# Softmax rows divided on GpSimd before the transposes, in a fused attention and two-layer MLP kernel with a planned instruction order

## The chip, the cores and the metric

The kernel runs on one core of a Trainium2 chip. A core has five engines with an instruction queue each: PE (TensorE: matmuls and transposes), DVE (VectorE), ACT (ScalarE), POOL (GpSimd) and SP (here it only issues DMAs). Each queue runs in order and the queues wait for each other by semaphores. The metric is device time in microseconds (us), lower is better.

## The reference, cut to what matters

```python
def _attn_ref(q, k, v):                        # batch 2, 12 heads, 448 tokens, head size 64
    scores = scale * np.matmul(q, k.transpose(0, 1, 3, 2))
    scores = np.where(mask, -1000000000.0, scores)          # causal
    scores = scores - np.max(scores, axis=-1, keepdims=True)
    attn = np.exp(scores)
    attn = attn / (np.sum(attn, axis=-1, keepdims=True) + 1e-09)
    return np.matmul(attn, v).astype(np.float32)

def reference(**kwargs):
    attn_out = _attn_ref(**attn_kwargs)
    x = attn_out.transpose(0, 2, 1, 3).reshape(B * S, H * D)          # 896 x 768
    x = _moe_ref(x=x, **moe_kwargs)      # (rational function of x @ w_in) @ w_out, 2048 wide
    return _moe2_ref(x=x, **moe2_kwargs) # (sigmoid(x @ w_gate) * (x @ w_val)) @ w_out, 1536 wide
```

All of it is float32, apart from weights that the kernel reads as double words and rounds itself.

## The kernel before, in words

**Attention.** Heads are taken two at a time: 12 pairs n = 0 to 11, six of each batch. The 448 query rows of a head are four tiles t of 112 rows, and a pair is worked off in three groups k: tiles 0 and 1, tile 2, tile 3. For each group PE multiplies queries by keys (`scores`, tile `s`, in PSUM), DVE takes the masked, negated row maximum and writes the scaled scores to SBUF (`maximum`, tile `e`, one instruction for each head of the pair), ACT makes the exponentials in place with the row sums beside them (`exponentials`, tile `sum`), PE transposes the 112 x 112 blocks (`turn`, tile `p`), DVE or ACT copies them from PSUM to SBUF (`copied`, tile `pt`), and PE multiplies them by the values (`values`, tile `x`). The tiles `s` and `p` share one ring of two PSUM buffers (`ps_s`), so each waits for the readers of the one before the last. A tile `e` has two buffers, one for each head, so `maximum` of pair n + 1 waits for the transposes of pair n.

**The softmax division before.** The exponentials are transposed and multiplied undivided. `inverses` turns the eight columns of `sum` of a pair into reciprocals on DVE, `factors` spreads them over PSUM with eight matmuls on PE (tile `r`, line 501), `factors_out` copies that tile to SBUF on ACT (line 511), and `result` multiplies `x` by it on DVE (line 528). Then ACT rounds the product to `xh` and the rest goes to `xl`: on POOL for ten pairs, on DVE for the last pair of each batch (line 540). `xh` and `xl` are what the MLP reads.

**The MLP.** Each product is made of three matmuls (high by high, low by high, high by low). Of the first layer the tiles `h` (x by w_in) and `o` (by w_out) of batch 0 stand between the attention's instructions on PE as filler: a tile `h` needs `xh` and `xl` of pair u for its u-th part. A weight portion of 128 x 768 comes by DMA (`raw`), passes two ACT steps, one of DVE (`val`, line 164) and two of POOL (`wh` or `oh`, line 172; `wl` or `ol`, line 176). From 130 us on, only MLP matmuls run on PE.

**What sets the order.** Every piece of work is a `Job` with an engine, a cost, what it depends on and a rank. `in_turn` plays the jobs through with these costs (an engine that comes free takes the ready job of lowest rank), and the kernel's instructions are put on each engine in that order, which is then fixed:

```python
        now, e = min((max(free[e], min(j.ready for j in w)), e) for e, w in waiting.items() if w)
        job = min((j for j in waiting[e] if j.ready <= now), key=lambda j: j.rank)
        waiting[e].remove(job)
        free[e] = now + job.cost
```

Of the kernel before, what the change touches and what calls it, by code (L numbers as in the profile page):

```python
# [8 lines left out]
F32 = mybir.dt.float32  # L9
# [16 lines left out]
class Job:  # L26


    def __init__(self, engine, cost, deps, rank, emit):
        self.engine, self.cost, self.rank, self.emit = engine, cost, rank, emit  # L30
        self.deps = deps
        self.ready = 0.0
        self.then = []


def in_turn(named, handoff):

    free = {}
    waiting = {}
# [30 lines left out]
def tile_causal_attention__moe_rational__moe_glu(  # L70
# [13 lines left out]
    nc = tc.nc  # L84
# [408 lines left out]

    def factors(n):

        d = T[n]
        d["r"] = ps_r.tile([P, 512], F32, tag="r", name=f"r_{n}")[:, :S]

        for i in range(NQ):
            for j in range(2):  # L500
                nc.tensor.matmul(
                    d["r"][j * D : (j + 1) * D, i * CP : (i + 1) * CP],
                    d["sum"][:, i, j : j + 1].to_broadcast([CP, D]),
                    ident[:CP, :CP],
                    start=True,
                    stop=True,
                )
# [49 lines left out]
    LA = 2  # L557
    R_TURN, R_R, R_X, R_W = -11.0, -16.0, 34.0, -3.5
    R_MAX, R_COPY, R_INV, R_XN = -14.5, -9.5, 7.0, 12.5
    R_EXP, R_ROUT = 6.25, -42.5  # L560
    W_AT, W_STEP = 9, 5
    R_SUM = 9.5
    EXP = (0.39, 0.48, 0.57, 0.67)
    MAX = (0.28, 0.39, 0.51, 0.62)
    COPY = (0.39, 0.62, 0.70, 1.09)
    both = range(2)
    for it in range(len(pairs) * NG + LA):
        n, k = divmod(it, NG)
        rank = it * NQ / NG
        if n < len(pairs):  # L570
            if k == 0:
                job(("load", n), "SP", 3.0, [("x", n - 3, NQ - 1)], (n - 2) * NQ, load, n)
            job(
                ("s", n, k),
                "PE",
                sum(0.187 * (t + 1) + 0.05 for t in GROUPS[k]) + 0.25,
                [("load", n), *freed_by("s")],
                rank - 37.5,
                scores,
                n,  # L580
                k,
            )
            for t in GROUPS[k]:
                for j in both:
                    job(("max", n, t, j), "DVE", MAX[t] + 0.08, [("s", n, k), ("p", n - 1, k)], rank + R_MAX, maximum, n, k, t, j)
                    job(("exp", n, t, j), "ACT", EXP[t] + 0.19, [("max", n, t, j), ("r", n - 3)], rank + R_EXP, exponentials, n, t, j)
# [15 lines left out]
        for t in GROUPS[k]:  # L602
            job(("copy", n, t), "ACT" if t == 2 else "DVE", COPY[t], [("p", n, k), ("x", n - 2, NQ - 1)], rank + R_COPY, copied, n, k, t)
        freed["s"].append([("copy", n, t) for t in GROUPS[k]])
        if k < NG - 1:
            continue
        job(("inv", n), "DVE", 0.4, [("exp", n, t, j) for t in range(NQ) for j in both], rank + R_INV, inverses, n)
        job(("r", n), "PE", 0.9, [("inv", n), ("r out", n - 1)], rank + R_R, factors, n)
        job(("r out", n), "ACT", 0.52, [("r", n), ("hi", n - 1), ("lo", n - 1)], rank + R_ROUT, factors_out, n)
        for kt in range(NQ):  # L610
            deps = [("copy", n, t) for t in range(kt, NQ)] + [("x", n, kt - 1) if kt else ("xn", n - 1)]
            job(("x", n, kt), "PE", 0.187 * (NQ - kt) + 0.15, deps, rank + R_X + kt / 2, values, n, kt)
        job(("xn", n), "DVE", 0.62, [("x", n, NQ - 1), ("r out", n)], rank + R_XN, result, n)
        job(("hi", n), "ACT", 0.57, [("xn", n)], rank + 1, result_hi, n)
        final = pairs[n][1] == NP - 1
        job(("lo", n), "DVE" if final else "POOL", 0.62 if final else 1.14, [("hi", n)], rank + 1, result_lo, n)


# [24 lines left out]

    STAGES = [("SP", 4.0), ("ACT", 0.92), ("ACT", 0.9), ("DVE", 1.3), ("ACT", 0.84), ("POOL", 2.0)]
    portions = []

    def portion(key, w, free, rank):
        p = len(portions)
        portions.append(key)
        for m, (engine, cost) in enumerate(STAGES):  # L650
# [9 lines left out]
            if not isinstance(rank, tuple):  # L660
                r = rank - 4 if m == 0 else rank + R_W
# [94 lines left out]
    def stage_out(c, b):  # L756
# [23 lines left out]
    def stage_out2(c, b):  # L780
# [113 lines left out]
```

## Time and profile before

| what | value |
|---|---|
| median of 3 runs | 603.45 us (603.12 to 603.87) |
| span of the profiled execution, first to last instruction | 601.4 us |
| PE busy | 593.5 us, 99% |
| DVE, ACT, POOL busy | 358.0 (60%), 357.2 (59%), 254.4 us (42%) |
| PE busy from 0 to 120 us | 115.63 us |
| DVE busy from 60 to 120 us | 54.21 us of 60 |

The profile shows one execution; its page gives the span and no total of its own, so its time is taken as the span and the 2.05 us by which the median exceeds it. The shares of the whole mix two stages: up to about 126 us attention, where four engines are loaded, and after it the MLP, where PE alone is full.

### The profile page before, as it was taken

Reading aid. Unit: us, or ns where it says so; the run is one execution under the profiler, and the core shown is the slowest. Engines: PE = TensorE matmul, PEld = TensorE weight load, DVE = VectorE, ACT = ScalarE, POOL = GpSimd, SP = SyncE. Lnnn points to the kernel's source line nnn. Section 1 sums busy time; section 2 is a strip of 40 time slices with the busy share of each in tenths; the row PEclk is TensorE's granted clock in tenths of the full one; section 3 lists DMA queues with packets and bytes.
Section 4 is the critical chain, followed back from the end, with each engine's and each line's share of the span. In section 5 each row is a group of like instructions: output and inputs, shape, how many; then the busy total and the mean of one; then the engine's idle time right before and its main releaser. Section 6 shows DMA issues by size and latency. Waiting matters only on the chain.

```text
span 601.4 us, 8821 instructions
## 1 busy us (share of the span) xinstructions
PE 593.5 (99%) x3352; PEld 511.6 (85%) x3352; DVE 358.0 (60%) x677; ACT 357.2 (59%) x686; POOL 254.4 (42%) x193
## 2 busy tenths in 40 slices
PE   7999999999999999999999999999999999999997
PEld 5566666689988998898898989989989989989987
DVE  5877899938968986789685243246336335312314
ACT  6888888858897793859396448766344444111010
POOL 0634321357529656534746465545145144211010
PEclk9999999999999999999999999999999999999999
DMA  7645340045413351323421054645324123000004
GB/s 242 207 173 158 118 166 16 6 157 166 146 53 110 108 195 53 113 88 123 152 59 51 2 158 158 210 157 161 102 105 159 54 105 106 0 1 1 0 14 170
DMA packets 25641, 65.05 MB, mean 108 GB/s; under 512 B 1984, under 2 KB 3776, under 8 KB 25600
## 3 DMA queue, kind: packets, MB, share of 16 engines
q1 hardware_dynamic: 25600, 64.50, 32.7%
q8 instruction: 26, 0.43, 0.3%
q14 instruction: 15, 0.12, 0.1%
HBM read 61.74 MB, written 2.75 MB: 107 GB/s over the span
## 4 chain that ended last, share of the span: by engine, by line
PE 97%; DVE 2%; issue 0%; ACT 0%; DVEq 0%
PE h L256 7%; PE o L314 6%; PE h L258 6%; PE h L257 6%; PE o L315 6%; PE o L316 6%; PE z L381 5%; PE z L379 5%; PE z L380 5%; PE gu L257 5%; PE gu L258 5%; PE gu L256 5%; PE vu L257 5%; PE vu L256 5%; PE vu L258 5%; PE s L442 4%
## 5 line engine op out<-in xcount | busy, mean ns | idle before, releaser
L361 POOL TENSOR_TENSOR gl<-pr_u,gh 128x384 fp32r<-128x384 f32 (+1 forms) x24 | 27.7, 1153 | 111.5 <-ACT gh L359 111.5
L289 POOL TENSOR_TENSOR gl_h<-t_h,gh_h 128x384 fp32r<-128x384 f32 (+2 forms) x32 | 39.2, 1226 | 84.0 <-ACT gh_h L287 83.9
L256 PE MATMUL h<-xh,wh_in 128*128 128x384 f32 (+2 forms) x192 | 71.3, 371 | 0.0
L314 PE MATMUL o<-gh_h,oh_out 128*128 128x384 f32 (+2 forms) x192 | 70.3, 366 | 0.0
L315 PE MATMUL o<-gl_h,oh_out 128*128 128x384 f32 (+2 forms) x192 | 69.9, 364 | 0.0
L316 PE MATMUL o<-gh_h,ol_out 128*128 128x384 f32 (+2 forms) x192 | 69.9, 364 | 0.0
L258 PE MATMUL h<-xh,wl_in 128*128 128x384 f32 (+2 forms) x192 | 69.7, 363 | 0.0
L257 PE MATMUL h<-xl,wh_in 128*128 128x384 f32 (+2 forms) x192 | 69.7, 363 | 0.0
L176 POOL TENSOR_TENSOR ol_out<-val_out,oh_out 128x768 fp32r<-128x768 f32 x28 | 55.1, 1971 | 26.7 <-ACT oh_out L174 25.4
L389 DVE TENSOR_TENSOR y<-y,z 128x384 f32<-128x384 f32 x70 | 38.3, 552 | 32.2 <-PE z L381 32.1
L357 DVE TENSOR_TENSOR pr_u<-sg_u,vu 128x384 f32<-128x384 f32 (+1 forms) x24 | 14.8, 617 | 70.8 <-PE vu L258 68.4
L381 PE MATMUL z<-oh_out,gl 128*128 128x384 f32 x168 | 56.2, 335 | 0.0
L379 PE MATMUL z<-oh_out,gh 128*128 128x384 f32 x168 | 56.2, 335 | 0.0
L380 PE MATMUL z<-ol_out,gh 128*128 128x384 f32 x168 | 56.2, 334 | 0.0
L164 DVE SCALAR_TENSOR_TENSOR val_out<-raw_out 128x768 uint32<-128x768 uint32 x28 | 35.7, 1277 | 31.3 <-ACT raw_out L161 23.4
L464 ACT ACTIVATE e<-e,sc 112x112 f32<-112x112 f32 (+3 forms) x96 | 49.7, 522 | 6.5 <-DVE sc L450 6.3
L258 PE MATMUL gu<-xh,wl_gate 128*128 128x384 f32 (+1 forms) x144 | 52.2, 363 | 0.0
L257 PE MATMUL gu<-xl,wh_gate 128*128 128x384 f32 (+1 forms) x144 | 52.2, 363 | 0.0
L257 PE MATMUL vu<-xl,wh_val 128*128 128x384 f32 (+1 forms) x144 | 52.1, 362 | 0.0
L256 PE MATMUL gu<-xh,wh_gate 128*128 128x384 f32 (+1 forms) x144 | 52.1, 362 | 0.0
L256 PE MATMUL vu<-xh,wh_val 128*128 128x384 f32 (+1 forms) x144 | 52.1, 362 | 0.0
L258 PE MATMUL vu<-xh,wl_val 128*128 128x384 f32 (+1 forms) x144 | 52.1, 362 | 0.0
(89 smaller groups left out, 1425.5 us busy)
## 6 DMA issues: line engine op xcount, KB each, us to landing
raw_out<-in_moe_w_out_dram SPq DMA_DIRECT2D x28, 768.0 KB, 4.3
raw_in<-in_moe_w_in_dram SPq DMA_DIRECT2D x16, 768.0 KB, 4.5
raw_gate<-in_moe_w_gate_dram SPq DMA_DIRECT2D x12, 768.0 KB, 4.3
raw_val<-in_moe_w_val_dram SPq DMA_DIRECT2D x12, 768.0 KB, 4.3
qk<-in_qk_dram SPq DMA_DIRECT2D x12, 448.0 KB, 5.7
v<-in_v_dram SPq DMA_DIRECT2D x12, 224.0 KB, 3.8
out_dram<-y SPq DMA_DIRECT2D x14, 192.0 KB, 1.8
a_sb<-in_moe_a_dram SPq DMA_DIRECT2D x1, 2.0 KB, 7.1
```

Source lines behind the costliest of these rows:

```text
L176: nc.gpsimd.tensor_tensor(lo, vf, hi, op=ALU.subtract)
L256: nc.tensor.matmul(ps, hi[:, c, fs], xh[:, c, bs], start=(c == 0), stop=False)
L257: nc.tensor.matmul(ps, hi[:, c, fs], xl[:, c, bs], start=False, stop=False)
L258: nc.tensor.matmul(ps, lo[:, c, fs], xh[:, c, bs], start=False, stop=(c == KC - 1))
L289: nc.gpsimd.tensor_tensor(gl, t, gh, op=ALU.subtract)
L314: nc.tensor.matmul(ps, hi[:, es], gh, start=(i == 0), stop=False)
L315: nc.tensor.matmul(ps, hi[:, es], gl, start=False, stop=False)
L316: nc.tensor.matmul(ps, lo[:, es], gh, start=False, stop=(i == NF - 1))
L379: nc.tensor.matmul(ps, gh[:, ms], hi[:, ns], start=(i == 0), stop=False)
L380: nc.tensor.matmul(ps, gh[:, ms], lo[:, ns], start=False, stop=False)
L381: nc.tensor.matmul(ps, gl[:, ms], hi[:, ns], start=False, stop=(i == NF2 - 1))
L464: nc.scalar.activation(e, e, AF.Exp, bias=d["sc"][:, t, j : j + 1], scale=-1.0, accum_out=d["sum"][:, t, j : j + 1])
```

## The change

The row sums are inverted group by group (`inverses(n, k)`: an addition and a reciprocal for 4, 2 and 2 columns), and a new function `normalised` multiplies each tile `e` in place by its rows' reciprocals on POOL, eight instructions for a pair, before PE transposes it. `factors`, `factors_out` and `result` are gone, `xh` and `xl` are made from the tile `x` in PSUM, `xl` always on DVE. The PSUM that `r` took gives `x` a second buffer. The planner adds a cost (`switch`) where PE goes over between instructions that use half the array's rows (`s`), half its columns (`x`) or all of it, and a rank penalty (`stay`) for doing so; all ranks, costs and handoff times are new.

```diff
-        job = min((j for j in waiting[e] if j.ready <= now), key=lambda j: j.rank)
+        job = min((j for j in waiting[e] if j.ready <= now), key=lambda j: j.rank + stay * (j.mode != mode.get(e)))
         waiting[e].remove(job)
-        free[e] = now + job.cost
+        free[e] = now + job.cost + switch * (job.mode != mode.get(e))
+        mode[e] = job.mode
...
-    ps_x = att.enter_context(tc.tile_pool(name="ps_x", bufs=1, space=PSUM))
-    ps_r = att.enter_context(tc.tile_pool(name="ps_r", bufs=1, space=PSUM))
+    ps_x = att.enter_context(tc.tile_pool(name="ps_x", bufs=2, space=PSUM))
...
-    def inverses(n):
-        rs = T[n]["sum"]
+    def inverses(n, k):
+        rs = T[n]["sum"][:, GROUPS[k][0] : GROUPS[k][-1] + 1]
         nc.vector.tensor_scalar_add(rs, rs, 1e-9)
         nc.vector.reciprocal(rs, rs)
+
+    def normalised(n, t, j):
+        e = T[n]["e", t, j]
+        nc.gpsimd.tensor_scalar(e, e, T[n]["sum"][:, t, j : j + 1], 1.0, op0=ALU.mult, op1=ALU.mult)
...
-    def factors_out(n):
-        T[n]["xn"] = xn_p.tile([P, S], F32, tag="xn", name=f"xn_{n}")
-        nc.scalar.copy(T[n]["xn"], T[n]["r"])
...
-    def result(n):
-        nc.vector.tensor_tensor(T[n]["xn"], T[n]["xn"], T[n]["x"], op=ALU.mult)
...
     def result_hi(n):
-        nc.scalar.copy(xh[x_part(n)], T[n]["xn"])
+        nc.scalar.copy(xh[x_part(n)], T[n]["x"])
 
     def result_lo(n):
-
-        eng = nc.vector if pairs[n][1] == NP - 1 else nc.gpsimd
-        eng.tensor_tensor(xl[x_part(n)], T[n]["xn"], xh[x_part(n)], op=ALU.subtract)
+        nc.vector.tensor_tensor(xl[x_part(n)], T[n]["x"], xh[x_part(n)], op=ALU.subtract)
...
+        job(("inv", n, k), "DVE", 0.31, [("exp", n, t, j) for t in GROUPS[k] for j in both], rank + R["inv"], inverses, n, k)
+        for t in GROUPS[k]:
+            for j in both:
+                job(("norm", n, t, j), "POOL", NORM[t] + C["norm"], [("inv", n, k)], rank + R["norm"], normalised, n, t, j)
         job(
             ("p", n, k),
             "PE",
-            sum(0.2 * (t + 1) for t in GROUPS[k]) + 0.1,
-            [("exp", n, t, j) for t in GROUPS[k] for j in both] + freed_by("s"),
-            rank + R_TURN,
+            sum(0.191 * (t + 1) for t in GROUPS[k]) + C["p"],
+            [("norm", n, t, j) for t in GROUPS[k] for j in both] + freed_by("s"),
+            rank + R["turn"],
```

PE, the start of the attention. In the rows `s_n_k` and `p_n_k` are scores and transposes of pair n, group k (a running number behind), and `e_n_t_j` the exponentials of tile t and head j. Before:

```order
L442 MATMUL s_0_2_178<-qk_0_0_143 112x448 x2
L482 MATMUL p_0_0_194<-ident_102,e_0_0_0_165 112x112
L482 MATMUL p_0_0_194<-ident_102,e_0_0_1_167 112x112
L482 MATMUL p_0_0_194<-ident_102,e_0_1_0_170 112x112 x2
L482 MATMUL p_0_0_194<-ident_102,e_0_1_1_173 112x112 x2
L442 MATMUL s_1_0_206<-qk_0_1_150 112x112 x2
L442 MATMUL s_1_0_206<-qk_0_1_150 112x224 x2
L482 MATMUL p_0_1_215<-ident_102,e_0_2_0_176 112x112 x3
L482 MATMUL p_0_1_215<-ident_102,e_0_2_1_188 112x112 x3
L442 MATMUL s_1_1_236<-qk_0_1_150 112x336 x2
L501 MATMUL r_0_243<-ident_102,sum_0_0_147 64x112 x8
```

The same place on PE in the changed kernel:

```order
L443 MATMUL s_0_2_175<-qk_0_0_140 112x448 x2
L443 MATMUL s_1_0_202<-qk_0_1_147 112x112 x2
L443 MATMUL s_1_0_202<-qk_0_1_147 112x224 x2
L487 MATMUL p_0_0_210<-ident_102,e_0_0_0_162 112x112
L487 MATMUL p_0_0_210<-ident_102,e_0_0_1_164 112x112
L487 MATMUL p_0_0_210<-ident_102,e_0_1_0_167 112x112 x2
L487 MATMUL p_0_0_210<-ident_102,e_0_1_1_170 112x112 x2
L487 MATMUL p_0_1_228<-ident_102,e_0_2_0_172 112x112 x3
L487 MATMUL p_0_1_228<-ident_102,e_0_2_1_178 112x112 x3
L443 MATMUL s_1_1_247<-qk_0_1_147 112x336 x2
```

The scores of pair 1 have moved ahead of the first transposes, and the tile `r` behind `s_1_1` is gone.

DVE, the same stretch. `ISA` rows are row maxima (the ones on `sc` read their result out), `COPY` takes the transposes out of PSUM. Before:

```order
L450 ISA e_0_3_0_192,sc_0_0_148<-s_0_2_178,mask_107 112x448
L450 ISA sc_0_0_148 112x1
L450 ISA e_0_3_1_201,sc_0_0_148<-s_0_2_178,mask_107 112x448
L450 ISA sc_0_0_148 112x1
L492 COPY pt_0_0_149<-p_0_0_194 112x2x112
L492 COPY pt_0_0_149<-p_0_0_194 112x2x2x112
L450 ISA e_1_0_0_222,sc_0_1_155<-s_1_0_206,mask_107 112x112
```

DVE there in the changed kernel:

```order
L471 TENSOR_SCALAR sum_0_0_144<-sum_0_0_144 112x4
L472 RECIPROCAL sum_0_0_144<-sum_0_0_144 112x4
L451 ISA e_0_3_1_194,sc_0_0_145<-s_0_2_175,mask_107 112x448
L451 ISA sc_0_0_145 112x1
L471 TENSOR_SCALAR sum_0_0_144<-sum_0_0_144 112x2
L472 RECIPROCAL sum_0_0_144<-sum_0_0_144 112x2
L471 TENSOR_SCALAR sum_0_0_144<-sum_0_0_144 112x2
L472 RECIPROCAL sum_0_0_144<-sum_0_0_144 112x2
L497 COPY pt_0_0_146<-p_0_0_210 112x2x112
L497 COPY pt_0_0_146<-p_0_0_210 112x2x2x112
L451 ISA e_1_0_0_226,sc_0_1_152<-s_1_0_202,mask_107 112x112
```

The three inversions of pair 0 stand between its last maxima and the copies, and the maxima of pair 1 still stand behind the copies of `p_0_0`.

POOL, where the first weight portions pass, in the changed kernel (before, the rows of `wh` and `wl` followed each other there, with one `xl` behind the second portion):

```order
L476 TENSOR_SCALAR e_1_2_1_264<-e_1_2_1_264,sum_0_1_151 112x336
L174 TENSOR_SCALAR wh_in0_0_312<-val_in0_0_0_301 128x768
L178 TENSOR_TENSOR wl_in0_0_313<-val_in0_0_0_301,wh_in0_0_312 128x768
L476 TENSOR_SCALAR e_1_3_0_286<-e_1_3_0_286,sum_0_1_151 112x448
L476 TENSOR_SCALAR e_1_3_1_291<-e_1_3_1_291,sum_0_1_151 112x448
L174 TENSOR_SCALAR wh_in0_0_312<-val_in0_0_3_349 128x768
L178 TENSOR_TENSOR wl_in0_0_313<-val_in0_0_3_349,wh_in0_0_312 128x768
L476 TENSOR_SCALAR e_2_0_0_326<-e_2_0_0_326,sum_0_2_185 112x112
```

The divisions of the exponentials now share POOL's queue with the weights, in turn. Over the attention as a whole, PE goes over between its three ways of using the array 111 times before and 94 times after; with the `r` tiles struck out of the order before, it is 96.

## Rows read from the trace of the kernel before

**Rows 1.** The page: busy time and share of each engine; the chain that ended last.

```profile
span 601.4 us, 8821 instructions
...
PE 593.5 (99%) x3352; PEld 511.6 (85%) x3352; DVE 358.0 (60%) x677; ACT 357.2 (59%) x686; POOL 254.4 (42%) x193
...
PE 97%; DVE 2%; issue 0%; ACT 0%; DVEq 0%
```

**Rows 2.** Busy time in three stretches: PE, PEld, DVE, ACT, POOL; clock, DMA share, GB/s.

```profile
0.00:20.00 20.00, 16.69 (x124) 11.13 (x124) 11.93 (x53) 14.24 (x40) 3.46 (x11) 1.00 0.60 192
20.00:60.00 40.00, 40.00 (x327) 24.15 (x324) 30.98 (x99) 34.17 (x99) 19.48 (x16) 1.00 0.58 196
60.00:120.00 60.00, 58.94 (x460) 38.13 (x456) 54.21 (x149) 50.49 (x134) 17.03 (x14) 1.00 0.23 77
```

**Rows 3.** Timeline of PE: start, duration, instructions; one `r` tile, and `x` split or whole.

```profile
67.03 0.99 PE L501 MATMUL r<-ident,sum 112*64 112x112 f32 x16
67.95 0.98 PE L482 MATMUL p<-ident,e 112*112 112x112 f32 x8
...
71.18 0.97 PE L519 MATMUL x<-pt,v 112*64 112x448 f32 x4
...
73.57 1.36 PE L519 MATMUL x<-pt,v 112*64 112x336 f32 x12
...
81.13 2.11 PE L519 MATMUL x<-pt,v 112*64 112x448 f32 x16
```

**Rows 4.** Groups by line, 0 to 130 us: count, busy us, mean ns, idle before.

```profile
L501 PE MATMUL r<-ident,sum 112*64 112x112 f32 x192 | 11.8, 266 | 0.1
L528 DVE TENSOR_TENSOR xn<-xn,x 128x448 f32<-128x448 f32 x12 | 7.4, 614 | 2.2 <-PE x L519 1.9 <-ACT xn L511 0.3
L540 POOL TENSOR_TENSOR xl<-xn,xh 128x448 fp32r<-128x448 f32 x10 | 12.9, 1290 | 19.5 <-ACT xh L535 19.5
L176 POOL TENSOR_TENSOR wl_in<-val_in,wh_in 128x768 fp32r<-128x768 f32 x6 | 11.6, 1932 | 0.5
L172 POOL TENSOR_SCALAR wh_in<-val_in 128x768 fp32r<-128x768 f32 x6 | 5.0, 835 | 31.4 <-DVE val_in L164 24.9 <-DMA raw_in<-in_moe_w_in_dram 6.5
```

**Rows 5.** Timeline of PE at the start of the attention, idle time before in brackets.

```profile
7.70 0.78 PE L482 MATMUL p<-ident,e 112*112 112x112 f32 x6
9.04 0.83 PE L442 MATMUL s<-qk 64*112 64x112 f32 x8 [0.56 <-DVE sc L450]
9.97 0.76 PE L482 MATMUL p<-ident,e 112*112 112x112 f32 x6
```

**Rows 6.** Timeline of DVE in the same stretch.

```profile
8.36 0.62 DVE L450 CUSTOM_DVE_ANT_0 e<-s,mask 112x448 f32<-112x448 f32 x1
...
8.91 0.92 DVE L492 COPY pt<-p 112x224 f32<-112x224 f32 x2
10.04 0.28 DVE L450 CUSTOM_DVE_ANT_0 e<-s,mask 112x112 f32<-112x112 f32 x1 [0.21 <-PE s L442]
...
11.05 0.17 DVE L470 TENSOR_SCALAR sum<-sum 112x8 f32<-112x8 f32 x1
...
11.37 0.12 DVE L624 TENSOR_SCALAR nb<-b_sb 128x2 f32<-128x2 f32 x1
```

**Rows 7.** Timelines of POOL and DVE at 64 us, the same moment.

```profile
64.45 1.83 POOL L176 TENSOR_TENSOR ol_out<-val_out,oh_out 128x768 fp32r<-128x768 f32 x1
...
64.54 1.77 DVE L470 TENSOR_SCALAR sum<-sum 112x8 f32<-112x8 f32 x1
```

**Rows 8.** Timelines of DVE, PE and POOL behind the attention, 125 to 149 us.

```profile
125.37 0.63 DVE L540 TENSOR_TENSOR xl<-xn,xh 128x448 fp32r<-128x448 f32 x1 [1.14 <-ACT xh L535]
...
134.06 0.37 PE L256 MATMUL h<-xh,wh_in 128*128 128x448 f32 x1
...
136.52 1.85 POOL L176 TENSOR_TENSOR wl_in<-val_in,wh_in 128x768 fp32r<-128x768 f32 x1
...
148.94 0.34 PE L256 MATMUL h<-xh,wh_in 128*128 128x384 f32 x1
```

More of the change, by code (lines that the diff above doesn't have):

```diff
@@ L26, with __init__ @@
 class Job:
-    def __init__(self, engine, cost, deps, rank, emit):
-        self.engine, self.cost, self.rank, self.emit = engine, cost, rank, emit
+    def __init__(self, engine, cost, deps, rank, emit, mode=None):
+        self.engine, self.cost, self.rank, self.emit, self.mode = engine, cost, rank, emit, mode
         self.deps = deps
@@ L33, in __init__, with in_turn @@
         self.then = []
-def in_turn(named, handoff):
+def in_turn(named, handoff, switch, stay):
     free = {}
+    mode = {}
     waiting = {}
@@ L492, in copied @@
             nc.vector.tensor_copy(dst, src)
[L494 to L507, printed above, removed]
-    def factors_out(n):
-        T[n]["xn"] = xn_p.tile([P, S], F32, tag="xn", name=f"xn_{n}")
-        nc.scalar.copy(T[n]["xn"], T[n]["r"])
     def values(n, kt):
@@ L557, in tile_causal_attention__moe_rational__moe_glu @@
     LA = 2
[L558 to L565, printed above, removed]
+    R = dict(s=-36.0, turn=-8.0, x=31.0, w=-5.0, max=-13.0, copy=-9.0, inv=-12.5, lo=20.0, norm=-4.0, hi=2.5, exp=8.25, sum=7.5)
+    C = dict(w_at=14.0, w_step=6.0, s=0.05, p=-0.08, x=-0.03, max=0.05, exp=0.07, switch=0.19, stay=1.0, norm=0.0, copy=0.12, wa=-0.02)
+    H = dict(PE=0.19, DVE=0.13, ACT=0.14, POOL=0.15, SP=0.15)
+    MODES = {"s": "rows", "x": "columns"}
+    EXP = (0.37, 0.465, 0.56, 0.65)
+    MAX = (0.195, 0.31, 0.425, 0.54)
+    NORM = (0.2, 0.32, 0.45, 0.57)
+    COPY = (0.30, 0.53, 0.60, 1.0)
     both = range(2)
@@ L575, in tile_causal_attention__moe_rational__moe_glu @@
                 "PE",
-                sum(0.187 * (t + 1) + 0.05 for t in GROUPS[k]) + 0.25,
+                sum(0.187 * (t + 1) + 0.0 for t in GROUPS[k]) + C["s"],
                 [("load", n), *freed_by("s")],
-                rank - 37.5,
+                rank + R["s"],
                 scores,
@@ L584, in tile_causal_attention__moe_rational__moe_glu @@
                 for j in both:
-                    job(("max", n, t, j), "DVE", MAX[t] + 0.08, [("s", n, k), ("p", n - 1, k)], rank + R_MAX, maximum, n, k, t, j)
-                    job(("exp", n, t, j), "ACT", EXP[t] + 0.19, [("max", n, t, j), ("r", n - 3)], rank + R_EXP, exponentials, n, t, j)
+                    job(("max", n, t, j), "DVE", MAX[t] + C["max"], [("s", n, k), ("p", n - 1, k)], rank + R["max"], maximum, n, k, t, j)
+                    job(("exp", n, t, j), "ACT", EXP[t] + C["exp"], [("max", n, t, j), *[("norm", n - 3, t, i) for i in both]], rank + R["exp"], exponentials, n, t, j)
             freed["s"].append([("max", n, t, j) for t in GROUPS[k] for j in both])
@@ L602, in tile_causal_attention__moe_rational__moe_glu @@
         for t in GROUPS[k]:
-            job(("copy", n, t), "ACT" if t == 2 else "DVE", COPY[t], [("p", n, k), ("x", n - 2, NQ - 1)], rank + R_COPY, copied, n, k, t)
+            job(("copy", n, t), "ACT" if t == 2 else "DVE", COPY[t] + C["copy"], [("p", n, k), ("x", n - 2, NQ - 1)], rank + R["copy"], copied, n, k, t)
         freed["s"].append([("copy", n, t) for t in GROUPS[k]])
@@ L606, in tile_causal_attention__moe_rational__moe_glu @@
             continue
-        job(("inv", n), "DVE", 0.4, [("exp", n, t, j) for t in range(NQ) for j in both], rank + R_INV, inverses, n)
-        job(("r", n), "PE", 0.9, [("inv", n), ("r out", n - 1)], rank + R_R, factors, n)
-        job(("r out", n), "ACT", 0.52, [("r", n), ("hi", n - 1), ("lo", n - 1)], rank + R_ROUT, factors_out, n)
         for kt in range(NQ):
[L611 to L616, printed above, removed]
+            deps = [("copy", n, t) for t in range(kt, NQ)] + [("x", n, kt - 1) if kt else ("lo", n - 2)]
+            job(("x", n, kt), "PE", 0.187 * (NQ - kt) + C["x"], deps, rank + R["x"] + kt / 2, values, n, kt)
+        job(("hi", n), "ACT", 0.42, [("x", n, NQ - 1)], rank + R["hi"], result_hi, n)
+        job(("lo", n), "DVE", 0.53, [("hi", n)], rank + R["lo"], result_lo, n)
     def coefficients():
@@ L642, in tile_causal_attention__moe_rational__moe_glu @@
     UNIT = {S: 0.615, CUT: 0.525, NT - CUT: 0.69}
-    STAGES = [("SP", 4.0), ("ACT", 0.92), ("ACT", 0.9), ("DVE", 1.3), ("ACT", 0.84), ("POOL", 2.0)]
+    STAGES = [("SP", 4.0), ("ACT", 0.79 + C["wa"]), ("ACT", 0.79 + C["wa"]), ("DVE", 1.1), ("ACT", 0.73 + C["wa"]), ("POOL", 1.9)]
     portions = []
@@ L660, in portion @@
             if not isinstance(rank, tuple):
[L661 removed]
+                r = rank - 4 if m == 0 else rank + R["w"]
             job((*key, m), engine, cost, deps, r, _spent, w)
@@ L733, in followed @@
         n_tmp.append((key, len(stages) - 1))
-    RATIONAL = [("ACT", 1.9), ("DVE", 2.0), ("ACT", 1.28), ("DVE", 2.05), ("ACT", 0.56), ("POOL", 1.3)]
-    GLU = [("ACT", 0.62), ("DVE", 0.62), ("ACT", 0.56), ("POOL", 1.25)]
+    RATIONAL = [("ACT", 1.56), ("DVE", 1.75), ("ACT", 1.17), ("DVE", 1.8), ("ACT", 0.46), ("POOL", 1.15)]
+    GLU = [("ACT", 0.44), ("DVE", 0.55), ("ACT", 0.48), ("POOL", 1.15)]
     def scaled(stages, c, b, more=0.0):
@@ L764, in stage_out @@
                 matmuls(key, i, deps + [("out", c, i, 0, 5), ("in", c, b, i, "after", 5)], UNIT[width(c, b)], out1_tile)
-            follow(key, scaled(stages, c, b, 0.15 * (c > 0) * b), at["end"] + R_SUM)
+            follow(key, scaled(stages, c, b, 0.15 * (c > 0) * b), at["end"] + R["sum"])
             yield
@@ L792, in stage_out2 @@
                     matmuls(key, i, deps + [("out2", c, i, 0, 5), *gs], UNIT2, out2_tile)
-                follow(key, stages, at["end"] + R_SUM)
+                follow(key, stages, at["end"] + R["sum"])
                 yield
@@ L837, in tile_causal_attention__moe_rational__moe_glu @@
     latest = {}
-    for j in in_turn(J, {"PE": 0.2, "DVE": 0.1, "ACT": 0.12, "POOL": 0.12, "SP": 0.1, "": 0.0}):
+    for j in in_turn(J, {**H, "": 0.0}, C["switch"], C["stay"]):
         traced = nc.cur_bb.bb.instructions
```

7 lines of the change are left out of this document (4 added, 3 removed).

## The prediction

> **What bounds the kernel now.** I read the page's busy shares and chain first: PE is busy 593.5 of 601.4 us, and 97% of the chain that ended last lies on PE [rows 1]. So work taken off PE shortens the kernel unless PE then waits. The second reading is where the other engines are close behind. By stretches, PE has no idle time from 20 to 60 us and 1.06 us from 60 to 120; DVE is busy 30.98 of 40 us and 54.21 of 60 there, 77% and 90%, ACT 85% and 84%, POOL 49% and 28% [rows 2]. The reader is to see that DVE is the next limit in the second half of the attention, and that the granted clock is full throughout (1.00, the 2.4 GHz level). After 120 us PE never waits until the tail, which the change leaves alone. All of its effect must come from the attention.
>
> **PE, removed.** An `r` tile starts at 67.03 and the transposes behind it at 67.95: 0.92 us for its eight matmuls, the change of array mode included [rows 3]. The group has 192 records, two for each of the 96 matmuls, so there are 12 such tiles [rows 4]. They are not hidden, since PE is the bound: 12 x 0.92 = **-11.0 us**. (The 11.8 us of that group are overlapping spans and would overstate it.)
>
> **PE, reordered.** The changes of mode fall from 111 to 94, but the order before has 96 once `r` is struck out, so the planner's new knowledge buys two. The price: a tile `x` in one piece spans 2.11 us, in two pieces 0.97 + 1.36 = 2.33 [rows 3], 0.2 us for a break. **-0.4 us.**
>
> **ACT, removed.** The copy of `r`. ACT is not the bound (85%), so this gives nothing by itself.
>
> **DVE, moved and added.** `result` goes: 12 instructions of 0.61 us, 7.4 us [rows 4]. Ten `xl` come from POOL; the one on DVE took 0.63 us [rows 8], 6.3 us. Inversions go from 12 to 36. One starts at 11.05 and the instruction behind it at 11.37, so 0.32 us [rows 6]; for fewer columns I take 0.3, which adds 24 x 0.3 = 7.2 us. Net: about +6 us on DVE. This costs nothing as long as PE's own work covers it; what cover is left is worked out below.
>
> **POOL, added.** 96 in-place multiplications, with a row factor from memory; the trace has none. Below: the multiplication by constants takes 835 ns for 768 columns, 1.08 ns a column [rows 4]. Above: the operation with two tensors takes 1932 ns, 2.5 ns a column [rows 4]. A pair has 2 x (112 + 224 + 336 + 448) = 2240 columns: 2.4 to 5.6 us. Only one tensor is streamed, so I stay near the lower row and allow 0.1 us more for each short instruction: 3.2 us a pair, 38 us in all. POOL loses 12.9 us of `xl` [rows 4] and goes from 40 to 65 us of the stage, which covers it. The Trainium skill, GPSIMD Engine Reference, section 4.1, speaks against this move: elementwise work is to stay on VectorE. In its section 3.1 a tight loop is given 1.8 cycles an element, 1.5 ns, by which I estimate 3.4 us a pair: the sum would stay as it is.
>
> **The start, where nothing fills PE.** Before, the first transposes begin at 7.70, DVE copies them from 8.91, takes the maxima of the next pair from 10.04 to 11.05, and PE's second transposes begin at 9.97 [rows 5, 6]. In the changed order DVE runs a maximum to 8.36, inverts group 0 (to 8.7), and POOL multiplies 672 columns: 0.7 us at the lower row, 1.7 at the upper, 1.1 taken. With a tenth for each handoff, the first transposes end at about 10.3. They ended at 8.48. The copies (0.85 us) and the next maxima (1.0 us) stand behind them on DVE, and the second transposes need the buffer that these maxima free: about 12.4 instead of 9.97. PE has the same two blocks between (1.5 us), so its idle time there grows from 0.8 to 3.2. Later small waits look alike in both orders. **+2.5 us**; 2.0 to 3.5 with the bounds of the multiplication.
>
> **The rest of the attention.** A pair's loop from maximum to transposes to the next pair's maximum is longer by an inversion and a multiplication, 0.4 + 1.1 us for a group, and PE's own time between two pairs shrinks by 0.9. The tile `e` has no spare buffer, so this comes out of slack: the next maximum, then the exponentials and transposes behind it are late if the slack is used up. DVE also gets blocked. At 64.54 the inversion's addition took 1.77 us instead of 0.17, up to the end of POOL's instruction that had started at 64.45 [rows 6, 7]. The Trainium skill, SBUF — State Buffer, section "Who interferes with whom", states the rule: a VectorE `tensor_scalar` in a two-port mode, or an instruction with two SBUF inputs, and a GpSimd instruction that reads SBUF shut each other out for its whole length. The trace agrees in that place. There are now 36 such additions, and POOL is busy over half of the stage. Going through the order, nine weight portions each leave an addition beside a `wh` or `wl`, with 0 to 1.2 us left of it, some 5 us together; short blocks by the new multiplications add perhaps 3. Some of this replaces blocks that the trace of before already has.
>
> DVE's sum: 97 us of work to 120 us [rows 2] + 6 + 6 = 109, on top of a start at 5.6 and some 3 us of waits in the first pairs: 118. PE's: 134.1 us to the first matmul of batch 1 in the next tiles [rows 8], less 11.4, plus 2.5: 125. DVE's last `xl` has to be done by then, and it leaves a margin of some 5%. With 10% spare, DVE cost PE 1.06 us in 60. At the same rate the 105 us would bring 1.9, 0.8 more than before; at twice the rate 3.7, 2.6 more. I take **+1.7 us**. The ends for this term are -1 (the waits of before go too) and +6 (half of 12 us of blocked DVE lands on PE).
>
> **Moved without a price.** The second `x` buffer: PE shows no wait for `result` at a tile `x`, so nothing. Weights behind the attention: POOL ends the last portion at 138.4 and PE needs it at 148.9 [rows 8]; the changed order leaves 30 instead of 51 filler matmuls behind the last `x`; at 0.207 us each (72 from 134.06 to 148.94) that is 4 us of the 10 us of slack, so nothing. DMAs keep their order in the attention.
>
> **Sum.** The profiled execution: 601.4 + 2.05 outside the span = 603.45, the median itself. 603.45 - 11.0 - 0.4 + 2.5 + 1.7 = 596.25, about **596.3 us**.
>
> **Rivals.**
>
> *The whole gain.* The start costs little, since DVE's idle time there takes it, and no wait grows: 603.45 - 11.4 - 1 + 1 = 592. For it: a PE without idle time from 20 to 60 us. Against it: the maxima behind the copies, which the order fixes.
>
> *DVE becomes the bound.* The blocked additions stand ahead of copies and maxima for which PE waits. At +6 us instead of +1.7: 600.6. For it: 90% before, and the 1.77 us row. Against it: at 90% DVE held PE up for 1 us only.
>
> *POOL is too slow (the other side).* If a row factor from memory costs what a second tensor costs, a pair takes 5.6 us, and in the first six pairs eight weight portions come on top: 8 x 2.77 / 6 = 3.7 us a pair. 9.3 us is more than the 8 to 9 us that PE has for a pair. Each of 36 groups gets its transposes 0.8 us later than taken; if 0.4 of that lands on PE, 14 us: 603.45 - 11.4 + 3.5 + 14 = 609. It decides from 0.25 us a group, which eats the net of 9 us. For it: the weight operations in the same queue. Against it: one tensor is read, not two.
>
> *The gain is given back.* PE reaches the next weights or the last `xl` sooner and waits there: no change, 602 to 604. Against it: the 10 us of slack.
>
> **Chances and range.** Forecast 0.5 (593.5 to 599.5), whole gain 0.17, DVE bound 0.2 (599.5 to 603), POOL too slow 0.08, given back 0.05. A measurement of this kernel tells 0.2% (1.2 us) from no change: faster is below 602.2, slower above 604.7. Faster: 0.5 + 0.17 + three quarters of 0.2 and a little of the last = 0.83; same 0.08; slower 0.09. The range of 591.0 to 602.3 leaves out POOL too slow, most of the gain given back, and the outer ends of DVE bound and of the whole gain, together about 0.2.
>
> **What would show it.** Right: no `r` on PE; PE busy about 11 us less up to the first matmul of batch 1; idle time of PE between 8 and 13 us of about 3 us, released by POOL and DVE; multiplications of 112 to 448 columns at 0.2 to 0.6 us. Wrong: multiplications near 1.1 us at 448 columns; additions of the inversion often above 0.5 us, and PE waiting for DVE all through the stage; a granted clock below 1.00 in the first 20 us, where PE's longer gaps are new; or PE waits behind the attention.

## The result and the profile after

The changed kernel takes 612.5 us (median of four runs, 610.9 to 613.6) beside 603.7 us of the kernel before on the same chip: a ratio of 1.0145 [1.0124, 1.0165]. It is slower by 1.2 to 1.7%, and outside the predicted range.

The page's busy times and chain, which answer to [rows 1], and the windows that answer to [rows 2]:

```profile
span 611.8 us, 8673 instructions
...
PE 595.0 (97%) x3160; PEld 506.9 (83%) x3160; DVE 365.3 (60%) x723; ACT 351.4 (57%) x674; POOL 294.9 (48%) x279
...
PEclk9899899699999999999999999999999999999999
...
PE 86%; DVE 8%; POOL 2%; issue 2%; ACT 2%; POOLq 0%; DVEq 0%; ACTq 0%
```

```profile
core 0: us, PE busy (x) PEld busy (x) DVE busy (x) ACT busy (x) POOL busy (x), PEclk, DMA share, GB/s
0.00:20.00 20.00, 15.83 (x72) 9.69 (x72) 10.24 (x47) 10.99 (x33) 7.69 (x23) 0.83 0.57 182
20.00:60.00 40.00, 36.48 (x244) 20.31 (x242) 37.20 (x109) 31.32 (x84) 31.86 (x44) 1.00 0.58 200
60.00:120.00 60.00, 54.48 (x325) 32.05 (x325) 53.03 (x162) 45.94 (x122) 36.43 (x50) 0.90 0.23 77
...
160.00:590.00 430.00, 429.98 (x2202) 394.73 (x2201) 232.10 (x343) 235.45 (x383) 194.93 (x141) 1.00 0.30 97
```

Two things are new. PE now waits: 3.52 us from 20 to 60 us, where it had no idle time, and 5.52 from 60 to 120, where it had 1.06; the chain gives 8% to DVE, where it gave 2%. And the granted clock is no longer 1.00: 0.83 in the first 20 us and 0.90 from 60 to 120, that is 0.17 x 20 x 2 = 6.8 us and 12 us at the lower level of 1.2 GHz. PE's busy time rises by 1.5 us (593.5 to 595.0) although its work falls, since part of it runs at half speed. From 160 to 590 us PE is as full as before. The first matmul of batch 1, at 134.06 before [rows 8], now starts here:

```profile
144.56 0.36 PE L258 MATMUL h<-xh,wh_in 128*128 128x448 f32 x1
```

That is 10.5 us later, as much as the span has grown (10.4). All of the loss lies in the attention. Of PE's idle time up to 130 us, the largest part is put down to maxima on DVE that come late (1.8 us before), and little to POOL itself (us in all, times, longest; a view of who came last, not of who made it late):

```profile
PE s L443 <- DVE sc L451: 4.8, 7, 1.5
...
PE p L487 <- POOL e L476: 1.1, 4, 0.4
```

The start on PE, which answers to [rows 5] (`s` scores, `p` transposes; idle time and releaser in brackets):

```profile
7.51 1.69 PE L443 MATMUL s<-qk 64*112 64x448 f32 x12 [0.77 <-DVE sc L451]
10.16 1.55 PE L487 MATMUL p<-ident,e 112*112 112x112 f32 x6 [0.96 <-DVE sum L471]
12.82 1.34 PE L487 MATMUL p<-ident,e 112*112 112x112 f32 x6 [1.11 <-DVE pt L497]
14.09 1.46 PE L443 MATMUL s<-qk 64*112 64x336 f32 x4
15.48 1.74 PE L487 MATMUL p<-ident,e 112*112 112x112 f32 x8
17.16 1.84 PE L443 MATMUL s<-qk 64*112 64x448 f32 x4
```

The three waits add up to 2.84 us. The first of them (0.77) was there before too (0.76, ahead of the same scores):

```profile
6.75 1.01 PE L442 MATMUL s<-qk 64*112 64x448 f32 x4 [0.76 <-DVE sc L450]
```

The first transposes take 1.55 us in place of 0.78 because they also wait for POOL between their matmuls (0.72 us on their weight loads); the granted clock is 1.00 from 10.1 to 11.8 us. From 12.82 on the same instructions take nearly twice their time: scores of 336 columns 1.46 us and of 448 columns 1.84, where the trace of before has 0.82 and 1.01.

The divisions, as the view of the tile `sum`, POOL's groups by shape and DVE's groups show them (duration in ns, minimum, median and maximum; then busy us and mean ns):

```profile
L476 POOL TENSOR_SCALAR e<-e,sum x96: 354/547/1855, 9.7 to 132.2; 112x112 f32<-112x112 f32 x24, 112x224 f32<-112x224 f32 x24, 112x336 f32<-112x336 f32 x24, 112x448 f32<-112x448 f32 x24
L471 DVE TENSOR_SCALAR sum<-sum x36: 139/166/2668, 9.1 to 131.0; 112x2 f32<-112x2 f32 x24, 112x4 f32<-112x4 f32 x12
L472 DVE RECIPROCAL sum<-sum x36: 165/166/179, 9.3 to 131.2; 112x2 f32<-112x2 f32 x24, 112x4 f32<-112x4 f32 x12
```

```profile
L476 POOL TENSOR_SCALAR e<-e,sum 112x448 f32<-112x448 f32 x24 | 15.8, 672 | 13.7 <-DVE sum L472 13.0 <-ACT xh L518 0.4 <-ACT raw_in L163 0.4
...
L476 POOL TENSOR_SCALAR e<-e,sum 112x112 f32<-112x112 f32 x24 | 9.7, 417 | 27.6 <-DVE sum L472 13.3 <-ACT e L465 7.7 <-PE s L443 3.1
...
L471 DVE TENSOR_SCALAR sum<-sum 112x2 f32<-112x2 f32 (+1 forms) x36 | 12.7, 352 | 1.1 <-ACT e L465 0.9
```

POOL spends 54.3 us on the 96 multiplications, 4.5 us a pair. The additions of 1e-9 (line 471) have a median of 0.166 us, a maximum of 2.67 and take 12.7 us together; the reciprocals behind them are never stretched.

How the three engines hold each other up is seen from 50 to 65 us. POOL, then DVE, then PE:

```profile
50.46 1.26 POOL L476 TENSOR_SCALAR e<-e,sum 112x448 f32<-112x448 f32 x2
51.68 1.83 POOL L178 TENSOR_TENSOR ol_out<-val_out,oh_out 128x768 fp32r<-128x768 f32 x1
...
56.19 1.55 POOL L476 TENSOR_SCALAR e<-e,sum 112x112 f32<-112x112 f32 x4 [0.94 <-DVE sum L472]
57.71 1.82 POOL L178 TENSOR_TENSOR ol_out<-val_out,oh_out 128x768 fp32r<-128x768 f32 x1
59.96 1.07 POOL L476 TENSOR_SCALAR e<-e,sum 112x336 f32<-112x336 f32 x2 [0.42 <-DVE sum L472]
```

```profile
48.62 0.95 DVE L166 SCALAR_TENSOR_TENSOR val_out<-raw_out 128x768 uint32<-128x768 uint32 x1
...
50.81 3.51 DVE L166 SCALAR_TENSOR_TENSOR val_out<-raw_out 128x768 uint32<-128x768 uint32 x1
54.25 0.61 DVE L521 TENSOR_TENSOR xl<-x,xh 128x448 fp32r<-128x448 f32 x1
...
56.90 2.67 DVE L471 TENSOR_SCALAR sum<-sum 112x2 f32<-112x2 f32 x1
59.60 0.17 DVE L472 RECIPROCAL sum<-sum 112x2 f32<-112x2 f32 x1
59.72 0.62 DVE L451 CUSTOM_DVE_ANT_0 e<-s,mask 112x448 f32<-112x448 f32 x1
```

```profile
54.91 0.47 PE L259 MATMUL h<-xl,wh_in 128*128 128x448 f32 x1 [1.71 <-DVE xl L521]
...
60.95 0.83 PE L443 MATMUL s<-qk 64*112 64x112 f32 x8 [1.48 <-DVE sc L451]
...
63.64 1.11 PE L487 MATMUL p<-ident,e 112*112 112x112 f32 x6 [1.14 <-DVE pt L497]
64.69 1.46 PE L443 MATMUL s<-qk 64*112 64x336 f32 x4
```

DVE's weight step `val`, which took 0.95 us at 48.62, starts at 50.81 and ends at 54.32, through two multiplications and the `ol` step of POOL (to 53.51); the `xl` behind it is late and PE waits 1.71 us. The addition at 56.90 ends with POOL's next `ol` step (59.53); the maximum behind it is late and PE waits 1.48 us, then 1.14. At 64.69 PE runs at half clock. The additions stretched here are the 1.77 us row of before [rows 7] over again, but now 36 of them meet a POOL that is busy for 31.86 of the 40 us from 20 to 60 (19.48 before).

### The profile page after: what moved, and what is told of

It reads as the page before. It is cut to its first block, busy times and chain, and to the rows that moved or that the text cites. A ratio compares the mean times of both kernels' runs of the same rounds, so it can differ in the third digit from the quotient of the medians.

```text
span 611.8 us, 8673 instructions
## 1 busy us (share of the span) xinstructions
PE 595.0 (97%) x3160; PEld 506.9 (83%) x3160; DVE 365.3 (60%) x723; ACT 351.4 (57%) x674; POOL 294.9 (48%) x279
## 4 chain that ended last, share of the span: by engine, by line
PE 86%; DVE 8%; POOL 2%; issue 2%; ACT 2%; POOLq 0%; DVEq 0%; ACTq 0%
PE o L316 6%; PE o L317 6%; PE o L318 6%; PE h L258 6%; PE h L260 6%; PE h L259 6%; PE z L382 5%; PE z L383 5%; PE z L381 5%; PE gu L260 5%; PE gu L259 5%; PE gu L258 5%; PE vu L260 5%; PE vu L259 5%; PE vu L258 5%; PE p L487 3%
## 5 line engine op out<-in xcount | busy, mean ns | idle before, releaser
L476 POOL TENSOR_SCALAR e<-e,sum 112x112 f32<-112x112 f32 (+3 forms) x96 | 54.3, 583 | 45.1 <-DVE sum L472 29.0
```

The costliest lines, as they stand in the source:

```text
L476: nc.gpsimd.tensor_scalar(e, e, T[n]["sum"][:, t, j : j + 1], 1.0, op0=ALU.mult, op1=ALU.mult)
```

## The experiments

All ran beside the kernel before, whose medians were 603.9 to 604.0 us. Where the planner is untouched, the order of all other instructions is that of the kernel named.

**Without the multiplications.** `normalised` issues nothing.

```diff
-        nc.gpsimd.tensor_scalar(e, e, T[n]["sum"][:, t, j : j + 1], 1.0, op0=ALU.mult, op1=ALU.mult)
```

> The changed kernel in its own order, with the 96 multiplications on POOL left out: the output is not divided by the row sums, the inversions still run on DVE. If POOL's division (its time in the loop, and DVE blocked by it) opens PE's gaps and the clock falls because of the gaps, then PE's idle time up to 130 us falls from 13 us to 6 or less, the granted clock stays at 1.00, and the kernel takes 592 to 597 us. If it is the planner's new order, or DVE, that opens the gaps, most of the idle time stays and it takes 606 us or more.

Measured: 599.8 us, 0.9939 [0.9924, 0.9954] of before, clock 0.996. The multiplications, with all that they hold up, are worth 12.7 us. Neither theory comes out whole. PE's idle time up to 130 us went from 13.2 to 9.9 us only, as the second had it; the time is 2.8 us above the first theory's range and 6.2 below the second's. The rest of the gain lies in PE's busy time (595.0 to 584.4 us), with less of it at half clock. The additions stay stretched without the multiplications, by what POOL still does, mostly weight steps, to 10.1 us in place of 36 x 0.166 = 6.0:

```profile
L471 DVE TENSOR_SCALAR sum<-sum 112x2 f32<-112x2 f32 (+1 forms) x36 | 10.1, 280 | 1.9 <-ACT e L465 1.8
```

**Without the additions.**

```diff
-        nc.vector.tensor_scalar_add(rs, rs, 1e-9)
```

> The changed kernel in its own order without the addition of 1e-9 to the row sums (a sum is at least 1, so float32 keeps none of it). If DVE held up in these 36 additions (12.5 us of DVE) is what PE waits for, the kernel gains 4 us or more: 608 us or less, with fewer stretches at half clock. If POOL's multiplications themselves or the order are what PE waits for, it stays within 2 us of 612.5.

Measured: 605.8 us, 1.0026 [1.0016, 1.0036]. In the first theory's range: 6.7 us for 36 instructions that do 6 us of work when nothing blocks them (36 x 0.166).

**PE filled in the start.** `filled` issues matmuls of constants into the tile `warm` ahead of the scores or transposes named.

```diff
+    FILL = {("p", 0, 0): 8, ("p", 0, 1): 10, ("s", 0, 2): 4, ("s", 1, 0): 4}
+    def filled(key):
+        for _ in range(FILL.get(key, 0)):
+            nc.tensor.matmul(warm[:, : 2 * P], ones[:, :P], ones, start=True, stop=True)
```

> The changed kernel with 26 matmuls more on PE (128 x 256, into a tile nobody reads) ahead of four waits in the first 13 us. If PE's gaps are what lets the clock fall, the stretch of 6.8 us at half clock from 12.8 us on goes away, the later ones stay, and the kernel takes about 609.5 us (6.8 us of busy PE at half speed cost 3.0 to 3.4 us). If the fall has another cause, the stretch stays and the time is 612 to 614 us.

Measured: 610.2 us, 1.0105 [1.009, 1.0121]; clock 1.00 from 0 to 20 us, where it was 0.83. 2.3 us gained by giving PE more work: with the gaps filled, the clock doesn't fall there.

**The planner's cost of a multiplication corrected.**

```diff
-    NORM = (0.2, 0.32, 0.45, 0.57)
+    NORM = (0.42, 0.63, 0.61, 0.67)
```

> The changed kernel with one line of the planner changed: its costs of a multiplication on POOL are the measured 0.42, 0.63, 0.61 and 0.67 us in place of 0.2, 0.32, 0.45 and 0.57. If the loss is an order built on too short a POOL, the order fitted to the real times brings back most of PE's waits and of the clock: 597 to 605 us. If the division on POOL is too slow in any order, 609 us or more.

Measured: 610.1 us, 1.0105 [1.009, 1.012]. In the second theory's range. The order that these costs give is 2.4 us better, no more.

**Without both.** The edits of the first two experiments together.

> The changed kernel in its own order with both left out, the additions of 1e-9 and the multiplications on POOL (the output is not divided by the row sums). The additions alone gave 6.7 us back, the multiplications alone 12.7. If they cost PE by two ways (a blocked DVE, and a loop that is longer by POOL's time) the gains add up: about 593 us. If POOL's multiplications cost mainly by blocking the additions, the second gain is within the first and the kernel stays at 598 to 600 us.

Measured: 595.5 us, 0.9864 [0.9841, 0.9888]. Behind the additions' 6.7 the multiplications give another 10.3; behind the multiplications' 12.7 the additions give 4.3. The time lies between the two forecasts: the gains add up for the most part, and overlap by 2.4 us. Its windows, and the start on PE:

```profile
0.00:20.00 20.00, 15.73 (x94) 10.33 (x96) 11.24 (x50) 12.94 (x37) 2.48 (x11) 0.91 0.60 184
20.00:60.00 40.00, 39.44 (x274) 22.53 (x269) 33.78 (x116) 35.71 (x100) 18.35 (x13) 1.00 0.66 228
60.00:120.00 60.00, 58.33 (x391) 38.51 (x391) 48.99 (x147) 50.06 (x131) 7.73 (x6) 1.00 0.25 84
```

```profile
6.98 1.69 PE L443 MATMUL s<-qk 64*112 64x448 f32 x12 [0.76 <-DVE sc L451]
9.42 0.76 PE L485 MATMUL p<-ident,e 112*112 112x112 f32 x6 [0.76 <-DVE sc L451]
11.50 1.34 PE L485 MATMUL p<-ident,e 112*112 112x112 f32 x6 [1.32 <-DVE pt L495]
```

The three waits of the start are here too, 2.84 us again, and behind them the clock falls for 0.09 x 20 x 2 = 3.6 us, with no multiplication and no addition in the kernel. So the rest of the change, its order above all, opens gaps in the start by itself.

**Another instruction in place of the addition.**

```diff
-        nc.vector.tensor_scalar_add(rs, rs, 1e-9)
+        nc.vector.reciprocal(junk[:, : len(GROUPS[k])], rs)
```

> The changed kernel in its own order, each addition replaced by one more reciprocal of the same columns into a tile nobody reads (0.16 to 0.18 us each in the trace of the changed kernel, never stretched; the addition takes 0.14 us when nothing blocks it). If it is the blocking by POOL's instructions that costs, the kernel comes close to the one without additions: 607.5 us or less. If 36 short instructions more on DVE, and their place ahead of the multiplications, cost that much by themselves, it stays at 609 us or more.

Measured: 608.9 us, 1.0078 [1.0058, 1.0098], between the two forecasts. The group of the new reciprocals:

```profile
L473 DVE RECIPROCAL junk<-sum 112x2 f32<-112x2 f32 (+1 forms) x36 | 5.8, 162 | 1.4 <-ACT e L465 1.1
```

They were never blocked, and 3.6 of the 6.7 us came back. So blocking is about half of the additions' cost (the interval of this time is 1.2 us to either side); 36 more short instructions in DVE's queue ahead of POOL's are the other 3.1.

**Multiplications off the path.** Without the additions; POOL's result goes to a tile nobody reads, here called `junk`.

```diff
-        nc.gpsimd.tensor_scalar(e, e, T[n]["sum"][:, t, j : j + 1], 1.0, op0=ALU.mult, op1=ALU.mult)
+        nc.gpsimd.tensor_scalar(junk, e, T[n]["sum"][:, t, j : j + 1], 1.0, op0=ALU.mult, op1=ALU.mult)
```

> The changed kernel in its own order without the additions, and with the 96 multiplications on POOL written to a tile nobody reads: POOL does the same work at the same time, the transposes take the undivided exponentials and don't wait for it (the output is not divided by the row sums). With the multiplications in the loop it was 605.8 us, without any 595.5. If they cost by standing between exponentials and transposes, the kernel takes 595 to 598 us. If they cost by blocking DVE's instructions and by the queue of weight steps behind them, it takes 602 us or more.

Measured: 599.1 us, 0.9909 [0.9892, 0.9925], between the two forecasts again. Of the 10.3 us, 3.6 remain when no transpose needs POOL's result, and 6.7 come from the place between exponentials and transposes. The cut isn't quite clean, since POOL still reads `e` and the next maxima overwrite it: 0.7 us of DVE's waits and 1.6 us of those of PE's weight loads are still put down to POOL. What POOL still does to DVE, by the group of `val_out`, in this kernel and in the one without both:

```profile
L166 DVE SCALAR_TENSOR_TENSOR val_out<-raw_out 128x768 uint32<-128x768 uint32 x4 | 7.6, 1908 | 0.1
```

```profile
L166 DVE SCALAR_TENSOR_TENSOR val_out<-raw_out 128x768 uint32<-128x768 uint32 x4 | 3.8, 956 | 0.3 <-issue 0.3
```

**The additions left out of the kernel before.**

> The kernel before without its 12 additions of 1e-9 (3.6 us of DVE, one of them blocked for 1.77 us). PE waits 1 us for DVE from 60 to 120 us, so a gain of at most 1 us: 603.0 to 603.9 us. If blocked additions hold PE up there too as in the changed kernel, about 0.19 us each, 601.7 us or less.

Measured: 603.9 us, 1.0001 [0.9992, 1.001]. They cost nothing there: there are 12 in place of 36, at the end of a pair, and no transpose waits for them.

**No modes in the planner.**

```diff
-    MODES = {"s": "rows", "x": "columns"}
+    MODES = {}
```

> The changed kernel with a planner that does not know PE's modes (all matmuls count as one mode; the order then has 96 changes of mode in place of 94). If the modes matter as little as forecast (0.2 us a change), it stays at 610 to 615 us, by chance of the order; if keeping modes together is what made the order worse, 608 us or less.

Measured: 613.8 us, 1.0167 [1.0151, 1.0182]. In the first forecast's range, as of an order shifted by chance; whether two changes of mode are worth 0.4 us can't be read from it.

**An order for the measured costs.** Without the additions; the cost of an inversion goes from 0.31 to 0.2, that of a `val` step from 1.1 to 1.3, and:

```diff
-    R = dict(s=-36.0, turn=-8.0, x=31.0, w=-5.0, max=-13.0, copy=-9.0, inv=-12.5, lo=20.0, norm=-4.0, hi=2.5, exp=8.25, sum=7.5)
+    R = dict(s=14.59, turn=-109.61, x=23.17, w=-6.56, max=-10.73, copy=-7.9, inv=-129.08, lo=22.63, norm=-2.9, hi=-51.29, exp=5.6, sum=62.47)
-    C = dict(w_at=14.0, w_step=6.0, s=0.05, p=-0.08, x=-0.03, max=0.05, exp=0.07, switch=0.19, stay=1.0, norm=0.0, copy=0.12, wa=-0.02)
+    C = dict(w_at=15.82, w_step=7.61, s=0.05, p=-0.08, x=-0.03, max=0.05, exp=0.07, switch=0.19, stay=5.07, norm=0.0, copy=0.12, wa=-0.02)
-    NORM = (0.2, 0.32, 0.45, 0.57)
+    NORM = (0.33, 0.43, 0.53, 0.63)
```

> The changed kernel without the additions, with the planner's costs as measured (multiplications 0.33, 0.43, 0.53 and 0.63 us, an inversion 0.2, a step of val 1.3) and ranks fitted anew to them. If an order built on costs that the chip does not keep is a part of the loss beside the additions, PE's idle time up to 130 us falls below 8 us and the kernel takes 599 to 603 us, below the 603.9 of before. If the loop over POOL costs this in any order, it stays at 604.5 us or more.

Measured: 603.1 us, 0.9976 [0.9964, 0.9988]. That is 0.1 us above the first theory's range and 0.9 below the kernel before, but PE still idles 10.8 us up to 120 us, where less than 8 was expected; the clock was 0.991 to 0.997, and the runs at 0.997 took 601.3 to 601.8 us, those at 0.991 603.2 to 604.0.

**The same with PE filled.** `filled` as above; ahead of the scores of pair 3 it writes into the `x` tile of pair 2, which the values overwrite behind it.

```diff
+    FILL = {("p", 0, 0): (None, 6), ("p", 0, 1): (None, 10), ("s", 0, 2): (None, 2), ("s", 1, 0): (None, 2), ("s", 3, 2): (2, 14)}
```

> The version without additions and with ranks fitted to the measured costs (603.1 us), with 34 matmuls more on PE into tiles nobody reads at that time, ahead of four waits in the first 13 us and of one of 1.9 us at 34 us. If the clock falls because of those gaps, both of its stretches at half clock (13 us, 34 us) go, and it takes 600 to 602 us at a clock of 1.00. If the clock costs nothing there because PE waits anyway, it stays at 602.5 to 604 us.

Measured: 600.5 us, 0.9938 [0.9924, 0.9953], clock 0.999 to 1.000. This beats both kernels. Its start:

```profile
9.95 0.98 PE L442 MATMUL warm<-ones 128*128 128x256 f32 x6
10.77 0.94 PE L498 MATMUL p<-ident,e 112*112 112x112 f32 x6
11.48 1.43 PE L442 MATMUL warm<-ones 128*128 128x256 f32 x10
12.82 0.76 PE L498 MATMUL p<-ident,e 112*112 112x112 f32 x6
13.73 0.82 PE L454 MATMUL s<-qk 64*112 64x336 f32 x4 [0.15 <-DVE sc L462]
14.48 0.98 PE L498 MATMUL p<-ident,e 112*112 112x112 f32 x8
```

The second transposes start at 12.82, as in the changed kernel to the hundredth: POOL's first multiplications start at 9.70 (9.69 there) and DVE's copies behind the first transposes at 11.75 in both, so the division is as late as ever. Only the matmuls behind are fast again, 0.82 and 0.98 us in place of 1.46 and 1.74.

**The changed kernel filled in three more places.** Its own order, additions kept.

```diff
+    FILL = {("p", 0, 0): (None, 8), ("p", 0, 1): (None, 10), ("s", 0, 2): (None, 4), ("s", 1, 0): (None, 4), ("s", 6, 0): (5, 10), ("s", 10, 1): (9, 4), ("s", 10, 2): (9, 11)}
```

> The changed kernel with 51 matmuls more, in the first 13 us and ahead of three waits at 58 and 105 to 110 us, where its clock still fell with the first filling. If gaps make the clock fall, it stays at 1.00 up to 130 us, and the kernel takes 607 to 609 us: the runs of the changed kernel at 0.992 and 0.983 differ by 2.7 us, so about 5 us in all hang on the clock, not the 10 us that 20 us at half clock would cost a PE that never waits. If the clock has another cause, it stays at 610 to 614 us.

Measured: 608.9 us, 1.008 [1.0049, 1.011]. Two runs kept a clock of 1.000 and took 607.1 and 607.3 us, as forecast; two at 0.993 took 610.6 and 610.7. The profiled one shows where it still falls, behind waits for POOL inside a group of transposes, which were not filled:

```profile
112.02 0.40 PE L499 MATMUL p<-ident,e 112*112 112x112 f32 x2 [0.51 <-POOL e L487]
112.81 0.62 PE L499 MATMUL p<-ident,e 112*112 112x112 f32 x2 [0.39 <-POOL e L487]
113.36 4.00 PE L517 MATMUL x<-pt,v 112*64 112x448 f32 x16
```

## Why the prediction was wrong

**In one sum.** Before 604.0; the order of the changed kernel without either operation 595.5, so -8.5; POOL's multiplications beside the loop +3.6; in the loop +6.7; the additions +6.7: 612.5. About 5 us of these 17, by estimate, are the clock (612.5 beside 607.2 in the filled runs at full clock), since a gap costs once as a wait and again behind it. At full clock the change is still 3 us slower than before. The shares depend on the order in which the parts are taken out, by 2.4 us.

**PE removed and reordered, -11.4: near.** 8.5 us show in the run without both operations, which keeps the rest of the change. Its PE is busy for 583.1 us, 10.4 less than before, although its clock in the first 20 us is 0.91; but PE idles 6.5 us up to 120 us, where it was 4.4 before.

**ACT, nothing: right.** It is less busy and nobody's bound. **The weights, nothing: right.** PE has no wait behind the attention. No run tried the second `x` buffer by itself.

**A multiplication, 3.2 us a pair: too small by a fifth.** Without a block, groups took 1.55 (as at 56.19), 1.07 and 1.26 us: 3.88 a pair, inside the bounds of 2.4 and 5.6; with blocks 4.5. The Trainium skill, GPSIMD Engine Reference, section 3.1, with its 1.8 cycles an element came out at 3.4 and nearer; its section 4.1, by which the operation belongs on VectorE, is not put to the test: no run here tried the operation there.

**The start, +2.5: the delay was near, partly by luck, and the clock was missing.** The second transposes start at 12.82, where 12.4 was forecast. But the first ones end at 11.71 (10.16 + 1.55), not at 10.3, and from there to the second ones it is 1.11 us, not 2.1: two misses that cancel. From the scores `s_0_2` to the second transposes it takes 5.31 us, where it took 3.22 before (6.75 to 9.97); the run without both operations takes 4.52, so 1.3 of the 2.1 us of delay come without addition and multiplication. What failed besides is that a wait was priced as its own length: filling the start gave 2.3 us back with the same 5.30 us from `s_0_2` to the second transposes. The fall of the clock stood in the list of what would make the prediction wrong, without a term or a chance. The Trainium skill, TensorE: Matmul & The Clock Gate, part 1, says that the clock is granted by how busy TensorE has lately been; the runs agree (1.00 in the start with filled gaps, 0.83 without).

**The rest of the attention, +1.7: the step that failed.** It took DVE's spare time as the measure ("at the same rate the 105 us would bring 1.9") and put the ends at -1 and +6. PE's idle time from 20 to 120 us went from 1.06 to 9.04 us. The blocked time itself was sized well: 8 us forecast, 5 of it by the weight steps; 12.7 - 36 x 0.166 = 6.7 us measured on the additions, and 10.1 - 6.0 = 4.1 without the multiplications. But an addition stands at the head of everything: POOL's multiplications, the transposes behind them, and on DVE's own queue the next maxima wait for it. The prediction saw that the loop grows by 0.4 + 1.1 us a group, but wrote "so this comes out of slack" and gave it no price of its own. In place of this term and that of the start, +4.2 together, the runs show +6.7 for the additions and +10.3 for the multiplications, 6.7 of these from their place in the loop (the run off the path) and 3.6 beside it; the clock's share is in both. The prediction also left out that the weight step `val` with its two SBUF inputs is blocked too (3.51 us at 50.81). The Trainium skill, SBUF — State Buffer, section "Who interferes with whom", names both kinds, and the trace agrees: additions up to 2.67 us, reciprocals never above 0.179.

**The planner.** The argument took the order as given and looked for single waits in it. It rests on costs that the chip doesn't keep (a pair on POOL 3.08 us planned, 3.88 at best). Its costs corrected gave 2.4 us with the additions; costs and ranks fitted anew gave 2.7 without them.

**The rivals.** "DVE becomes the bound" had the mechanism of the additions, and its +6 us is a third of the 17 that the two operations cost. "POOL is too slow" had nearly the time (609; its terms add up to 609.6), by a multiplication of 5.6 us a pair that takes 3.9. Neither let the two act together, and neither had the clock.

## What to carry to other kernels

An operation taken off the bound engine and put on others is paid for in the loop it joins: count the latency from producer to consumer through every in-order queue, not the spare busy time of the engine that takes it. An addition that changes no bit (1e-9 on a sum of at least 1) can be worth a percent when it stands at the head of such a loop and can be blocked by a neighbour. And where PE's full clock hangs on its being busy, price each new gap twice, or fill it: 34 matmuls that compute nothing took the refitted kernel from 603.1 to 600.5 us.

## What the runs showed of the hardware that was not expected

- In two places a blocked DVE instruction did not get its turn between two POOL instructions: `val` at 50.81 (0.95 us when free) waited through two multiplications and an `ol` step, 3.51 us, and the addition at 56.90 (median 0.166 us) through the end of the multiplications and the next `ol` step, 2.67 us.
- POOL's multiplication by a row factor in place grows little with its columns: 417 ns mean for 112 and 672 for 448, blocked ones included. Four of 112 and 224 columns took 1.55 us (at 56.19), two of 448 1.26 us (at 50.46).
- PE can run at half clock while it never idles: the three rows from 14.09 us on (scores, transposes, scores) follow each other without a wait, and each takes about 1.8 times what it takes at full clock (1.46, 1.74 and 1.84 us beside 0.82, 0.98 and 1.01).
